# One 2 MB weight load cut into eight spread pieces, and the second group's loads held back behind a transpose

## The chip, the core and the metric

The kernel runs on one core of one Trainium2 chip. The metric is the device time of one execution in microseconds (us), as the median of several executions; for a program on one core that is the time of this core. The engines are TensorE (PE in the profile; PEld is its weight loads), VectorE (DVE), ScalarE (ACT), GpSimd (POOL), and SyncE (SP), whose queue issues nearly all transfers here. Every execution also reports the mean granted TensorE clock, 1.000 being full speed.

## The reference, cut to what matters

Two attention blocks with 2048 tokens, width 1024 and 32 heads, put side by side. Block A is plain softmax attention; block B goes over four segments of 512 tokens with a causal mask, plus a memory that is carried from segment to segment.

```python
qkv = x @ wqkv; p = softmax(q @ k.T * Dh**-0.5); a = (p @ v) @ wo          # A
for s in range(4):                                                          # B
    a_dot = softmax(qs @ ks.T * scale + mask) @ vs
    a_mem = (phi(qs) @ M) / (phi(qs) @ z + 1e-6)
    outs.append(g * a_mem + (1 - g) * a_dot)
    M, z = M + phi(ks).T @ vs, z + phi(ks).sum()
b = concat(outs) @ wo_B
return concat([a, b], axis=-1)
```

## The kernel before

The program does not fix the order of its instructions by hand. Work is described as many small processes; at build, a scheduler plays them against a **model of times** and writes down, for each engine, the order in which the model ran its instructions. That order is then static on the chip. The model has a clock for the transfer queue, too: a transfer of `kb` kilobytes holds it for kb/230 us and is taken to have landed 1.7 us later.

```python
def dispatch(self, eng, t):                  # the scheduler, at build; cut
    ...
    if rq.kb:
        self.dma_free = max(self.dma_free, start + min(cost, 0.6)) + rq.kb / 230
        op.end = max(start + cost, self.dma_free) + 1.7
    ...

def load_WoB(self):                          # B's output weights, before
    yield ("ev", ("pos", self.par["wob"]))   # wob = 60: after 60 steps of the attention
    yield do("SP", lambda e: e.dma_start(self.WoB[:, :, :], self.B_wo.rearrange("(j p) n -> p j n", p=P)),
             w=[("WoB", j) for j in range(NG)], cost=0.6, prio=6, kb=2048)
    self.Q.fire("WoB")
```

The tile WoB serves first as room for early exponentials, so its weights cannot come at the start. `load_WA` and `load_WB` bring 256 KB of projection weights for the next group of heads, `load_xB` 512 rows of B's input through a transposing transfer, and `turn` transposes a V tile (into VA or VB) or the key features of B (into PKt) on the same queue. PKt is read by the matmuls that update the memory (line 942 before, 944 after). The exponentials are line 1112 before, 1114 after; the score matmuls that they wait for are line 1081, then 1083; the matmuls with V are line 1227, then 1229.

## Time and profile before

| what | before |
|---|---|
| median of 3 runs, then of 6 | 1103.65 us, then 1102.97 us |
| all six | 1099.79 to 1105.68 us |
| profiled execution: span, mean clock | 1105.1 us, 0.992 |
| ACT busy, idle | 1078.1 us, 27.0 us |
| WoB load: size, to landing | 2048 KB, 11.7 us |

Idle time of ACT is what there is to win: the span is ACT's busy time plus its idle time.

### The profile page before, as it was taken

The page shows a single profiled execution, that of the slowest core. Times are in us where ns is not written, and L with a number is a line of the kernel's source. Part 1 is how long each engine was busy: PE and PEld are TensorE (multiplying, and loading weights), DVE is VectorE, ACT ScalarE, POOL GpSimd, SP SyncE. Part 2 cuts the span into 40 slices and gives each one's busy share as a digit, 9 for nine tenths or more (in the row PEclk, how much of TensorE's full clock was granted, in tenths as well). Part 3 has the DMA queues.
Part 4 walks back from the last instruction along what each step waited for, and adds up shares of the span by engine and source line. Part 5 has one row for each costly group of instructions (what it writes and reads, how often), then busy time and mean ns, then how long its engine had stood idle before and what let it go on. Part 6 is the DMA issues. An engine that isn't in the chain of part 4 may idle for free.

```text
span 1105.1 us, 54825 instructions
## 1 busy us (share of the span) xinstructions
PE 1045.0 (95%) x25518; PEld 542.3 (49%) x25518; DVE 750.4 (68%) x1573; ACT 1078.1 (98%) x1188; POOL 126.0 (11%) x231
## 2 busy tenths in 40 slices
PE   8899899999999989999999999999999998999998
PEld 4554454544545445454454444445454554554554
DVE  2366547565786978888888798977757768543334
ACT  6999899999999999999999999999999999999997
POOL 2011101101011021110102112211111111100000
PEclk9999899999999999999999999999999999999999
DMA  9722522234302222243212132341142121201011
GB/s 192 98 60 56 126 65 51 53 72 74 74 22 55 61 55 50 46 84 70 60 37 60 36 70 55 65 79 37 46 70 55 37 55 27 84 32 36 32 41 66
DMA packets 213770, 67.53 MB, mean 61 GB/s; under 512 B 202787, under 2 KB 210979, under 8 KB 213539
## 3 DMA queue, kind: packets, MB, share of 16 engines
q1 hardware_dynamic: 212066, 63.07, 27.3%
q8 instruction: 201, 3.29, 1.3%
q10 hardware_dynamic: 1472, 0.92, 0.3%
q14 instruction: 31, 0.25, 0.1%
HBM read 36.70 MB, written 8.39 MB: 41 GB/s over the span
## 4 chain that ended last, share of the span: by engine, by line
ACT 67%; PE 26%; DVE 4%; DMA 1%; issue 1%; ACTq 0%; DVEq 0%
ACT PT L1112 66%; PE ps L726 12%; PE ps L1227 6%; PE ps L1081 5%; PE ps L1322 2%; DMA WA<-in_A_wqkv_dram 1%; DVE OD L1275 1%; ACT OTA L1112 1%; DMA VA<-VT 0%; DVE VT L731 0%; DVE PT L1122 0%; DMA VB<-VT 0%; DVE PH L1150 0%; DVE we L1149 0%; ACT OTB L1112 0%
## 5 line engine op out<-in xcount | busy, mean ns | idle before, releaser
L1112 ACT ACTIVATE PT<-ps 128x1024 bf16<-128x1024 f32 x1164 | 1056.9, 1166 | 10.4 <-PE ps L1081 9.7
L1227 PE MATMUL ps<-PT,ones 128*32 128x256 bf16 (+2 forms) x4784 | 284.1, 269 | 0.0
L1227 PE MATMUL ps<-PT,VA 128*32 128x256 bf16 x4016 | 241.6, 274 | 5.1 <-issue 2.4
L1081 PE MATMUL ps<-QA,KA 32*128 32x256 bf16 x4096 | 211.1, 274 | 30.2 <-ACT PT L1112 25.3
L726 PE MATMUL ps<-xA,WA 128*32 128x512 bf16 (+2 forms) x3424 | 204.9, 359 | 3.9 <-issue 1.3
L726 PE MATMUL ps<-xB,WB 128*32 128x512 bf16 (+1 forms) x3120 | 205.8, 380 | 2.8 <-DVE KA L731 0.8
L1081 PEld LDWEIGHTS ps<-QA,KA 32*128 32x128 bf16 x4096 | 62.9, 92 | 203.6 <-ACT PT L1112 188.1
L1227 PEld LDWEIGHTS ps<-PT,ones 128*32 128x32 bf16 x4784 | 128.4, 97 | 32.0 <-issue 16.4
L1227 PEld LDWEIGHTS ps<-PT,VA 128*32 128x32 bf16 x4016 | 107.4, 96 | 41.2 <-issue 22.8
L726 PEld LDWEIGHTS ps<-xA,WA 128*32 128x32 bf16 x3424 | 77.0, 96 | 78.5 <-issue 28.5
L726 PEld LDWEIGHTS ps<-xB,WB 128*32 128x32 bf16 x3120 | 71.8, 96 | 76.9 <-issue 32.4
L1275 DVE COPY OD<-ps 128x512 f32<-128x512 f32 x127 | 86.7, 683 | 29.5 <-PE ps L1227 28.7
L731 DVE CAST VT<-ps 128x512 bf16<-128x512 f32 x64 | 44.1, 689 | 75.6 <-PE ps L726 68.4
L1327 DVE CAST outsb<-ps 128x512 bf16<-128x512 f32 x56 | 38.7, 690 | 79.1 <-PE ps L1322 76.9
L1124 POOL TENSOR_TENSOR PT<-PT,mask 128x256 bf16<-128x256 bf16 x64 | 46.7, 730 | 352.3 <-ACT PT L1112 351.3
L731 DVE CAST KQB<-ps 128x512 bf16<-128x512 f32 x64 | 44.0, 687 | 44.1 <-PE ps L726 43.8
L1322 PE MATMUL ps<-WoB,OTB 128*32 128x512 bf16 (+1 forms) x1044 | 67.6, 377 | 0.5 <-DVE KQB L731 0.4
L868 POOL COPY VZ<-VB 64x256 bf16<-64x256 bf16 x64 | 29.8, 465 | 318.3 <-DMA VB<-VT 284.2
L1281 DVE STREAM_TRANSPOSE OD<-Rall 128x256 f32<-128x256 f32 x127 | 55.8, 440 | 2.9
L1278 DVE STREAM_TRANSPOSE Dt<-OD 128x256 f32<-128x256 f32 x127 | 55.3, 437 | 2.3
L1322 PE MATMUL ps<-xA,OTA 128*32 128x512 bf16 x836 | 53.3, 379 | 0.0
L1227 PE MATMUL ps<-PT,VB 128*32 128x192 bf16 (+2 forms) x768 | 45.7, 245 | 6.5 <-DVE OD L1275 4.5
(111 smaller groups left out, 888.3 us busy)
## 6 DMA issues: line engine op xcount, KB each, us to landing
WB<-in_B_wk_dram SPq DMA_DIRECT2D x32, 256.0 KB, 3.0
WB<-in_B_wq_dram SPq DMA_DIRECT2D x32, 256.0 KB, 2.9
WB<-in_B_wv_dram SPq DMA_DIRECT2D x32, 256.0 KB, 3.3
out_dram<-outsb SPq DMA_DIRECT2D x63, 128.0 KB, 1.8
WA<-in_A_wqkv_dram SPq DMA_DIRECT2D x23, 256.0 KB, 3.2
WoB<-in_B_wo_dram SPq DMA_DIRECT2D x1, 2048.0 KB, 11.7
xA<-in_A_wo_dram SPq DMA_DIRECT2D x1, 2048.0 KB, 9.5
OTA<-in_A_x_dram SPq DMA_DIRECT2D x2, 256.0 KB, 4.7
```

What stands on the lines that cost most here:

```text
L726: ins = e.matmul(self.ps[32 * c:32 * c + 32, bank, lo:hi], W[:, i, 32 * c:32 * c + 32], x(i)[:, lo:hi], start=st, stop=sp)
L731: return e.tensor_copy(dst, self.ps[:, bank, 0:n])
L868: yield do("POOL", lambda e, j=j: e.tensor_copy(self.VZ[H * j:H * j + H, j:4:2, :], V[0:H, j:4:2, 0:P]), r=[("VB", n % 2)], w=["VZ"], cost ...
L1081: ins = e.matmul(out, l, r, start=a, stop=z)
L1112: yield do("ACT", lambda e: e.activation(to, self.ps[:, pr[0]:pr[1] + 1, 0:n], ACTF.Exp, scale=sc), r=[("ps", bk) for bk in pr], w=keys, c ...
L1124: yield do("POOL", lambda e: e.tensor_tensor(d, d, m, ALU.mult), r=keys + ["mask"], w=keys, cost=0.4 + sz * 0.0014, prio=0)
L1227: ins = e.matmul(out, l, r, start=st, stop=sp)
L1275: yield do("DVE", lambda e: e.tensor_copy(OD[:, :], self.ps[:, OB, :]), r=[("ps", OB)], w=[("OD", x), ("Rb", x)], cost=dve(2 * QU), prio=0 ...
L1278: yield do("DVE", lambda e: e.transpose(Dt[:, :], Rb), r=[("Rb", x)], w=[("Dt", x)], cost=dve(QU), prio=self.par["fp"], hold=0.15)
L1281: yield do("DVE", lambda e: e.transpose(Rb.rearrange("p (a b) -> p a b", b=32), self.spread(Rc)), r=[("Rc", ui % 64)], w=[("Rb", x)], cost ...
L1322: ins = e.matmul(self.ps[32 * c:32 * c + 32, bank, lo:hi], lhs(j)[:, 32 * c:32 * c + 32], W(j)[:, lo:hi], start=st, stop=sp)
L1327: return f(self.outsb[ob][:, :], self.ps[:, bank, :])
```

## The change

Its intent is to keep the transfer queue from filling up: WoB comes in eight pieces of 256 KB, six steps apart, and the loads of the second group, with B's first ones, wait until the last V transpose of the first group has been issued.

```diff
-    par = dict(..., wob=60, mg=0.05, ...)
+    par = dict(..., wob=60, wobs=6, mg=0.05, ...)
-    def load_WA(self, k, g, prio=5, via="SP"):
+    def load_WA(self, k, g, prio=5, via="SP", after=None):
+        if after:
+            yield ("ev", after)
...
-                Q.spawn(self.load_WA(k, g + 1))
+                Q.spawn(self.load_WA(k, g + 1, after=("VA", 0, 3)))
...
     def load_WoB(self):
-        yield ("ev", ("pos", self.par["wob"]))
-        yield do("SP", lambda e: e.dma_start(self.WoB[:, :, :], ...), w=[("WoB", j) for j in range(NG)], cost=0.6, prio=6, kb=2048)
+        src = self.B_wo.rearrange("(j p) n -> p j n", p=P)
+        for j in range(NG):
+            yield ("ev", ("pos", self.par["wob"] + self.par["wobs"] * j))
+            yield do("SP", lambda e, j=j: e.dma_start(self.WoB[:, j, :], src[:, j, :]), w=[("WoB", j)], cost=0.6, prio=6, kb=256)
         self.Q.fire("WoB")
...
         def later():
             yield ("ev", ("pos", self.par["bpos"]))
+            yield ("ev", ("VA", 0, 3))
             for k in range(3):
                 yield from self.load_WB(k, 0)
```

More of the change, by code (lines that the diff above doesn't have):

```diff
@@ L405 @@
 class Kernel:
-    par = dict(b=(16, 12, 9), mem=0, memM=2, span=60, rate=0.6, ahead=28, sl=7, pv=14, ob=4, lead=6, b0=1, bpos=16, wob=60, mg=0.05, off=0, oks=(1, 4, 6), sh=4, pd=6, o0=4, od=0, run=4, po=(1, 1), fp=2, fil=0.65, fs=0.15, ta=2, td=40, pvw=3, pvs=3, slk=0.2, pat=0.0, kh=3, xp=0, wm=1, mk=(0, 1, 1), mp=0, pe=3, tk=(0.5, 1))
+    par = dict(b=(16, 12, 9), mem=0, memM=2, span=60, rate=0.6, ahead=28, sl=7, pv=14, ob=4, lead=6, b0=1, bpos=16, wob=60, wobs=6, mg=0.05, off=0, oks=(1, 4, 6), sh=4, pd=6, o0=4, od=0, run=4, po=(1, 1), fp=2, fil=0.65, fs=0.15, ta=2, td=40, pvw=3, pvs=3, slk=0.2, pat=0.0, kh=3, xp=0, wm=1, mk=(0, 1, 1), mp=0, pe=3, tk=(0.5, 1))
     def __init__(self, nc, A_x, A_wqkv, A_wo, B_x, B_wq, B_wk, B_wv, B_wo, B_beta, out):
@@ L1579, in load_WoB @@
     def load_WoB(self):
-        yield ("ev", ("pos", self.par["wob"]))
-        yield do("SP", lambda e: e.dma_start(self.WoB[:, :, :], self.B_wo.rearrange("(j p) n -> p j n", p=P)),
-                 w=[("WoB", j) for j in range(NG)], cost=0.6, prio=6, kb=2048)
+        src = self.B_wo.rearrange("(j p) n -> p j n", p=P)
+        for j in range(NG):
+            yield ("ev", ("pos", self.par["wob"] + self.par["wobs"] * j))
+            yield do("SP", lambda e, j=j: e.dma_start(self.WoB[:, j, :], src[:, j, :]), w=[("WoB", j)], cost=0.6, prio=6, kb=256)
         self.Q.fire("WoB")
```

## The prediction

The forecast's sum: 5.45 + 0.91 - 0.8 = 5.56 us off 1103.65, which gave 1098.1.

> **What bounds the kernel now.** I read the page first (busy time, chain, costliest groups), then the list of who waited for whom on ScalarE (ACT), then the timeline around each ACT gap, then a table of stretches and the DMA view for the same microseconds.
>
> ```profile
> PE 1045.0 (95%) x25518; PEld 542.3 (49%) x25518; DVE 750.4 (68%) x1573; ACT 1078.1 (98%) x1188; POOL 126.0 (11%) x231
> ...
> ACT 67%; PE 26%; DVE 4%; DMA 1%; issue 1%; ACTq 0%; DVEq 0%
> ...
> L1112 ACT ACTIVATE PT<-ps 128x1024 bf16<-128x1024 f32 x1164 | 1056.9, 1166 | 10.4 <-PE ps L1081 9.7
> ```
>
> ACT is busy 1078.1 of a span of 1105.1 us, nearly all of it in the exponentials of line 1112. The third line says that its own idle time before those 1164 instructions is only 10.4 us, so the most that any change of loads can win is small. The chain names TensorE (PE) for 26%, because PE is 95% busy and the two take turns, but ACT is the one that hardly ever stops. All ACT idle is 1105.1 - 1078.1 = 27.0 us. From the timeline: the start holds 2.51 + 5.53 + 1.90 + 0.35 = 10.3 us (first loads), the end about 6.2 us (last projections and the last store). That leaves about 10.5 us in the middle, and the two places that the change touches hold most of it. First place, the ACT timeline (start, length, last column idle before it):
>
> ```profile
> 123.56 3.08 ACT L1112 ACTIVATE PT<-ps 128x1024 bf16<-128x1024 f32 x3
> 129.80 3.40 ACT L1112 ACTIVATE PT<-ps 128x1024 bf16<-128x1024 f32 x4 [3.15 <-PE ps L1081]
> 133.96 1.94 ACT L1112 ACTIVATE PT<-ps 128x1024 bf16<-128x1024 f32 x2 [0.76 <-PE ps L1081]
> 136.37 3.89 ACT L1112 ACTIVATE PT<-ps 128x1024 bf16<-128x1024 f32 x4 [0.47 <-PE ps L1081]
> 141.34 9.39 ACT L1112 ACTIVATE PT<-ps 128x1024 bf16<-128x1024 f32 x10 [1.07 <-PE ps L1081]
> ```
>
> The exponential before the second line ended at 126.65; ACT then stands 3.15 us, and again 0.76, 0.47 and 1.07 until 141.34: 5.45 us together. All of them wait for score matmuls of line 1081. Why these were late, from the timeline of all engines:
>
> ```profile
> 117.80 0.69 SPq L1581 DMA_DIRECT2D WoB<-in_B_wo_dram  x1
> ...
> 125.06 0.28 PE L1227 MATMUL ps<-PT,VA 128*32 128x256 bf16 x2
> ...
> 127.53 1.85 SPq L737 DMA_TRANSPOSE VA<-VT  x1
> 127.74 0.40 PE L1227 MATMUL ps<-PT,VA 128*32 128x256 bf16 x2 [2.40 <-issue]
> ```
>
> Line 1581 is the one 2 MB load of B's output weights (WoB). Seven and a half microseconds later PE stands 2.40 us inside a group of four matmuls that the program issues with no wait between them, only ahead of the first. So no buffer and no transfer of data is being waited for: the profile calls it "issue", and I read it as PE having no next instruction. The stretches (columns: PE, weight loads, VectorE, ACT, GpSimd busy; granted clock; DMA share; GB/s) show what goes with it:
>
> ```profile
> 118.00:121.00 3.00, 3.00 (x88) 1.78 (x84) 2.93 (x5) 3.00 (x5) 1.30 (x2) 1.00 1.09 226
> 121.00:124.00 3.00, 3.00 (x84) 1.68 (x72) 0.10 (x1) 3.00 (x5) 0.00 (x0) 1.00 0.94 338
> 124.00:127.50 3.50, 1.34 (x34) 0.61 (x31) 0.69 (x1) 2.65 (x3) 1.33 (x2) 0.96 1.18 345
> 127.50:132.00 4.50, 3.29 (x63) 2.27 (x65) 2.45 (x7) 2.20 (x3) 0.28 (x1) 0.50 1.05 59
> 132.00:136.00 4.00, 3.20 (x76) 1.42 (x68) 2.45 (x6) 3.14 (x4) 0.22 (x1) 0.50 0.00 1
> 136.00:142.00 6.00, 6.00 (x116) 2.61 (x112) 3.07 (x9) 4.54 (x5) 0.00 (x0) 0.59 0.01 3
> 142.00:150.00 8.00, 8.00 (x212) 4.61 (x200) 2.78 (x6) 7.98 (x10) 0.00 (x0) 1.00 0.39 86
> ```
>
> DMA is full from 118 to beyond 127.5, up to 345 GB/s. PE does 1.34 us of work in 3.50. Then the granted clock is 0.50 for over 8 us, where the same matmuls take longer (0.61 us for a batch of eight score matmuls against 0.40), and ACT gets 2.20 of 4.50, 3.14 of 4.00, 4.54 of 6.00. From 142 on all is as before. The DMA view of 112 to 140 us:
>
> ```profile
> q8 instruction: 4, 0.07, 1.0%
> ...
> WoB<-in_B_wo_dram SPq DMA_DIRECT2D x1, 2048.0 KB, 11.7
> ...
> WB<-in_B_wk_dram SPq DMA_DIRECT2D x1, 256.0 KB, 11.1
> ```
>
> Another 256 KB load of that window took 11.1 us to land, against a median of 3.0 for its kind on the page. Second place, the first V:
>
> ```profile
> 32.55 0.38 SPq L532 DMA_DIRECT2D WA<-in_A_wqkv_dram  x1
> ...
> 33.28 1.19 SPq L737 DMA_TRANSPOSE VA<-VT  x1
> ...
> 38.26 0.29 PE L1227 MATMUL ps<-PT,VA 128*32 128x256 bf16 x4 [1.13 <-DMA VA<-VT]
> ```
>
> The second group's WA load is put ahead of the last transpose of the first V, more loads follow it, the transpose takes 4.84 us to land (a piece of the chain) instead of the 2.4 of the fastest of its kind, and PE stands 1.13 us for it at 38.26. ACT's next exponential starts 0.91 us late (38.93).
>
> [...]201 packets of 3.29 MB on the instruction queue, 16.4 KB each. [...]the trace shows only that DMA was full when PE stood still. [...](2048 KB in 11.7 us, eight times 256 KB at 3.0 us would be 24), but rate is not what is short here. [...]
>
> **The change part by part.** (1) WoB in eight. Removed: one issue of 0.69 us on the sync queue. Added: eight of about 0.4 to 0.6 us (as the WB loads, 0.37 to 0.58), on a queue that only issues transfers. Bytes are the same. The pieces go at positions 60, 66, ..., 102. A position is two exponentials, bar those of B: 60 positions had passed at 117.8 us, and the whole order has 64 x 8 + 32 x 3 = 608 positions in about 1090 us, 1.79 us each; so one piece each 11 us and the last at 117.8 + 42 x 1.79 = 193 us. WoB is first read at 287.2 us: 90 us to spare. Each piece should land in some 3 us. What it takes off the path: the stop at 125 us (3.15) and the half clock after it (2.30), 5.45 us of ACT. Since every engine's order is fixed at build, what ACT gains at 141 us stays gained unless a later wait takes it. (2) The holding back. The WA load at 32.55 and the WB and xB loads of later wait for the issue of the last V transpose (33.28), so they move by a microsecond or less. The transpose then lands nearer 2.4 to 3.5 us, before 37 us, when PE has finished its earlier work (36.85 + 0.28). Gain 0.91 us of ACT. xB lands about 49 us and its user has no gap near it, so a microsecond there is free. Both parts together: 5.45 + 0.91 = 6.36 us, from 1103.65 to 1097.3. I take back 0.8 us for new small collisions (below): 1098.1.
>
> **Rivals.** (a) The stall stays. At position 60 the first piece still goes out together with three loads of 256 KB and two transposes within 6 us; if these alone starve PE, the time stays near 1102.7 (only part 2 pays). Against it: the load of A's output weights at 950 us is also 2 MB, lands in 9.5 us, and ACT is busy 22.00 of 22.00 us from 948 to 970. So a load of 2 MB alone is survived, and it takes 2 MB plus the bunch; with 256 KB in its stead the bunch is 1 MB. I give this 12%. (b) The pieces hit others. Eight more loads of 3 us among the transposes of V, whose landing PE waits for; each such hit could cost up to the 0.91 seen at 38 us, and two or three of them 2 us: about 1099.5. Some 20%. (c) The order moves. The program places instructions by its own model of engine and DMA times at build; another load plan there changes the order of PE and VectorE work after 117 us. ACT has 2.13 us of gaps at 396 to 401 us behind VectorE, and gaps of such kind may vanish or arise: plus or minus 2 us. (d) PE is the real bound, and the 5.45 us would come back as waits on PE. Against it: from 142 us on ACT stands still for 0.16 us only until 300 us, although PE had fallen behind by the same stop.
>
> **Range and chances.** The floor is busy time plus start and end, 1078.1 + 10.3 + 6.2 = 1094.6 of span, about 1093 for the median, which was 1.5 below the span. The other side is rival (a) with noise: the three runs of before spread from 1099.79 to 1105.68. So 1093.5 to 1102.8 holds it 8 times in 10. Faster by over 2% would need 22 us, more than ACT can give: 1%. Slower by over 2% would need a stall that nothing hints at: 1%.
>
> **What would show it.** Right: no ACT gap over 0.5 us between 100 and 200 us, the granted clock 1.00 there, no PE stop by "issue" inside a group, eight WoB loads with a median landing near 3 us, and no ACT gap at 38 us; ACT busy still about 1078 and its idle time near 20 to 21 us. Wrong: the gap near 125 us with only one piece under way (rival a), fresh gaps behind VA or VB transposes (b), or gaps at other places behind VectorE (c). The prediction is wrong above all if the PE stop has nothing to do with the load.

## The result, and the profile after

The changed kernel took 1101.97 us (median of 6, 1100.72 to 1104.20) against 1102.97 for the kernel before. The ratio is 0.9993, with a 95% interval of 0.9974 to 1.0013. A ratio here is the mean time of one kernel's fast runs over that of the other's in the same rounds, so it is not quite the ratio of the medians. Of the 5.5 us that I forecast not more than about 1 is there.

And yet the profile after looks just as it was predicted to. From the page of the changed kernel (busy times; the chain that ended last; the exponentials with the idle time before them):

```profile
PE 1038.3 (94%) x25434; PEld 539.3 (49%) x25434; DVE 749.2 (68%) x1573; ACT 1078.1 (98%) x1188; POOL 126.1 (11%) x231
...
ACT 62%; PE 27%; DVE 8%; DMA 3%; issue 1%; SPq 0%; DVEq 0%
...
L1114 ACT ACTIVATE PT<-ps 128x1024 bf16<-128x1024 f32 x1164 | 1056.8, 1165 | 4.5 <-PE ps L1083 3.8
```

ACT is busy 1078.1 us as before, and its idle time before exponentials fell from 10.4 to 4.5 us. The span is 1099.0, which is 6.1 less. The stretches around the first WoB piece (columns: stretch, length, busy PE, PEld, DVE, ACT, POOL, granted clock, DMA share, GB/s):

```profile
124.00:127.50 3.50, 3.10 (x88) 1.88 (x84) 2.81 (x7) 3.50 (x6) 1.37 (x3) 1.00 0.20 42
127.50:132.00 4.50, 4.17 (x104) 1.84 (x96) 3.55 (x9) 4.50 (x7) 0.38 (x1) 1.00 0.49 120
132.00:136.00 4.00, 3.79 (x108) 1.95 (x104) 3.37 (x8) 4.00 (x5) 0.00 (x0) 1.00 0.46 101
```

PE works 3.10 of 3.50 us where it had worked 1.34, ACT all of them, the clock stays at 1.00 and DMA is at a half or less. Comparing these two profiles would have told the predicted story to the end: 6.1 us gained. The timed runs of the same two kernels say otherwise. So the question for the experiments is which of the two profiles is not typical, and what else differs.

### The profile page after: what moved, and what is told of

The parts are those of the page before. It is cut to its first block, busy times and chain, and to the rows that moved or that the text cites. A ratio compares the mean times of both kernels' runs of the same rounds, so it can differ in the third digit from the quotient of the medians.

```text
span 1099.0 us, 54671 instructions
## 1 busy us (share of the span) xinstructions
PE 1038.3 (94%) x25434; PEld 539.3 (49%) x25434; DVE 749.2 (68%) x1573; ACT 1078.1 (98%) x1188; POOL 126.1 (11%) x231
## 4 chain that ended last, share of the span: by engine, by line
ACT 62%; PE 27%; DVE 8%; DMA 3%; issue 1%; SPq 0%; DVEq 0%
ACT PT L1114 61%; PE ps L728 11%; PE ps L1229 6%; PE ps L1083 5%; PE ps L1324 3%; DMA xB<-in_B_x_dram 1%; DMA VA<-VT 1%; DMA PKt<-PH 1%; DVE VT L733 1%; DVE PH L1152 1%; DVE we L1151 1%; DVE PH L899 1%; DVE OD L1277 1%; DVE we L1150 1%; ACT OTA L1114 1%
## 5 line engine op out<-in xcount | busy, mean ns | idle before, releaser
L728 PE MATMUL ps<-xB,WB 128*32 128x512 bf16 x3096 | 203.6, 379 | 3.6 <-DMA xB<-in_B_x_dram 1.1
```

Source lines behind the costliest of these rows:

```text
L728: ins = e.matmul(self.ps[32 * c:32 * c + 32, bank, lo:hi], W[:, i, 32 * c:32 * c + 32], x(i)[:, lo:hi], start=st, stop=sp)
```

## The experiments

Twelve runs were made on the chip, all beside runs of the kernel before. **Theory 1** is the prediction's: the stop of PE near 125 us belongs to the 2 MB load and comes in every execution. **Theory 2**: its length is a matter of chance, and the profile that I read had caught a long one. A third possibility, the prediction's rival (c), is that the changed load plan makes the build write a different order, and that this order costs something elsewhere (theory A below).

### Is the stop always there? The kernel before once more, and each half alone

b_again is the kernel before, a_again the changed one. split_only leaves out the two lines of holding back; hold_only keeps them and puts the one 2 MB load back. The orders were compared instruction by instruction: hold_only has exactly the order of the kernel before on PE, ACT, DVE and POOL, split_only exactly that of the changed kernel. Only the transfers differ within each pair.

```diff
# split_only, against the changed kernel
-                Q.spawn(self.load_WA(k, g + 1, after=("VA", 0, 3)))
+                Q.spawn(self.load_WA(k, g + 1))
-            yield ("ev", ("VA", 0, 3))
# hold_only, against the changed kernel: load_WoB as before (one load, kb=2048)
```

> The kernel before once more, to see whether the 2.40 us stop of PE near 125 us and the half clock after it are there in every execution. Theory 1 (the stop belongs to the load and comes every time): every run shows a mean granted clock near 0.992, the profile shows ACT gaps of about 5.4 us between 126 and 142 us, ratio 1.000. Theory 2 (the stop is a matter of chance and comes in some executions): clocks of the runs differ, from 0.992 to 0.998, the time falls as the clock rises, and the profile may lack the gap.

> The changed kernel once more. Theory 1: clock 0.997 to 0.998 in all runs, no ACT gap over 1 us after 25 us, ratio to before 0.994 to 0.995. Theory 2 (chance stops in both): the mean ratio stays near 0.999, with runs of 1099 to 1100 at clock 0.998 and runs of 1102 to 1104 at 0.995, which means that other stops than the one of the load come in this kernel too.

> The eight spread pieces alone, without the holding back. The order of PE, ACT and DVE is the same as in the changed kernel, only the sync queue differs. Both theories: the ACT gap of about 0.9 us at 38 us is back and adds 0.9 us to the changed kernel. Theory 1: ratio to before 0.995. Theory 2: ratio 1.000 within 0.002.

> The holding back alone, with the one load of 2 MB. Both theories: no ACT gap at 38 us, 0.9 us less than before, ratio 0.999. Theory 1: the stop near 125 us is there in the profile and the clock is 0.992 in every run. Theory 2: the clocks of the runs differ as with the kernel before.

| run | median, range (us) | ratio to before, 95% | clocks of its runs |
|---|---|---|---|
| b_again | 1101.00, 1099.51 to 1105.21 | 1.0002, 0.9975 to 1.0030 | 0.994 to 1.000 |
| a_again | 1101.43, 1100.28 to 1102.44 | 0.9997, 0.9972 to 1.0022 | 0.997 to 0.998 |
| split_only | 1101.88, 1099.78 to 1103.58 | 1.0003, 0.9977 to 1.0029 | 0.995 to 0.998 |
| hold_only | 1098.94, 1097.34 to 1103.05 | 0.9974, 0.9948 to 1.0000 | 0.995 to 1.000 |

Theory 1 falls. The kernel before has runs of 1099.5 us at clock 1.000 and runs of 1105.2 at 0.994, and in these rounds one of 1108.28 at 0.992. The clocks can be read as a count: in the profiles the clock records show 0.50 for 3.41 us (once in the changed kernel's), or for two or four times that in one piece (6.8 us in hold_only, 13.65 in the first profile), and one such stretch lowers a mean over 1100 us by 0.0016. By an estimate from these numbers 0.998 means one stretch, 0.997 two, 0.995 three, 0.994 four and 0.992 five. Of the 39 runs of the kernel before in this set of rounds and the two below, the five with none took 1099.75 us in the mean, the six with four 1104.97. The profile that I had read has five, four of them in one piece from 127.25 us, at the stop.

Two expectations missed as well. The gap at 38 us was to come back in split_only with 0.9 us and to be absent in hold_only; from 35 to 41 us ACT lacked 0.31 us in the one and 0.62 in the other. And hold_only's 0.26% is three times the 0.9 us expected, at the edge of noise; it was not followed up.

The second profile of the kernel before has a span of 1097.8, less than the changed kernel's. Here is the place of the stop in that second profile (start, length, instruction, idle before it):

```profile
126.23 0.29 PE L1227 MATMUL ps<-PT,VA 128*32 128x256 bf16 x2 [0.32 <-issue]
...
127.44 1.02 ACT L1112 ACTIVATE PT<-ps 128x1024 bf16<-128x1024 f32 x1 [0.22 <-PE ps L1081]
```

PE stands again, inside the same group of four matmuls, but for 0.32 us instead of 2.40; ACT loses 0.22 us instead of 5.45, and the clock does not drop. hold_only, with the same order and the same load, stood 1.7 us there. The reading as a missing next instruction can be checked in the traces' own records. Counted in order of start, PE stops after its instruction 5825 in each of these three. An instruction block of 16 KB as the instruction queue moves it (201 packets, 3.29 MB) was close to 256 instructions (51262 PE instructions in 201 blocks), and 5825 is 22 x 256 + 193. Short stops at 11 and 16 us (0.72 and 0.58 us in the first profile) come after instructions 449 = 256 + 193 and 705 = 2 x 256 + 193. So these stops of PE are where, by this count, one block ends and the next begins. When was the missing block moved? From the DMA view of the kernel before, in the first profile, 121 to 125 us (the whole count of packets, then the queue of ordinary transfers; the instruction queue, q8, has no line at all):

```profile
DMA packets 693, 1.42 MB, mean 355 GB/s; under 512 B 0, under 2 KB 0, under 8 KB 693
...
q1 hardware_dynamic: 693, 1.42, 97.2%
```

And the next 1.5 us:

```profile
q1 hardware_dynamic: 629, 0.52, 104.2%
q8 instruction: 1, 0.02, 4.4%
```

While 1.42 MB went by, no instruction packet did; one is recorded at 125.17 us, when PE had already started its last instruction before the stop (125.06). When it was asked for the trace does not show. Over all profiles the picture is the same. The previous block was used up (instruction 5569) near 120 us; from there to the start of the fetch it took 5.12, 3.27 and 3.27 us in three profiles of the kernel before (the third is the single look below) and 4.59 in hold_only, against 0.66 to 1.23 us in the eight profiles of kernels with the spread load (over all 200 block ends of the first profile the median is 0.56 us). This block lasted PE 5.0 us in the first profile. After the delays of 0.66 to 1.23 us no stop is seen at its end, after those of 3.3 to 5.1 us stops of 0.6 to 2.7 us between two instructions' starts. What decides between 3.3 and 5.1 was not found. A last profile of the kernel before, alone, was taken to see one more stop:

> One more profile of the kernel before, for the length of the PE stop after its instruction 5825 (so far 2.67, 0.59 and, with the holding back, 1.98 us from one start to the next). If its length is a matter of chance between executions[...], it will again be another: somewhere from 0 to 3 us, with a fetch of the next block that starts 2 to 5.5 us after the block before was used up, against 0.7 to 1.2 us in all kernels with the spread load.

It took 1100.09 us and stopped 0.61 us at that place. So in three profiles of the kernel before, the loss of ACT between 100 and 160 us was 5.49, 0.22 and 0.24 us, and 2.77 in hold_only: 2.2 us in the mean of four, not 5.45.

Theory 2 explains the first profile. It does not explain why the changed kernel, which has that stop in no profile, isn't at 1099. hold_only, which may have it, is even the faster. The order is left.

### Order and load taken apart

The order was frozen: the scheduler still sees one transfer of 2048 KB and so writes the order of the kernel before, and only afterwards the load is cut, with pieces 1 to 7 put 12 exponentials apart. That is split_old_order, and hold_split_old_order with the holding back. one_new_order does the reverse: the changed kernel's order, but the first piece brings all 2 MB at once (the later ones are cut to 16 KB each; the result is right). load_more puts 1.5 MB of useless loads ahead of the 2 MB one. All four were checked to have exactly the order of PE, ACT, DVE and POOL that they claim.

```diff
# split_old_order, against the kernel before (deps and semaphores of the new pieces cut)
+        self.wob_op = yield do("SP", lambda e: e.dma_start(self.WoB[:, 0, :], src[:, 0, :]), w=[...], cost=0.6, prio=6, kb=2048)
+    def spread_WoB(self):                    # called when the order is complete
+        acts = [o for o in R.all[i0:] if o.ex == "ACT"]
+        for j in range(1, NG):
+            o = Op(f"D{23 + j}", 0, lambda e, j=j: e.dma_start(self.WoB[:, j, :], src[:, j, :]))
+            R.all.insert(R.all.index(acts[12 * j - 1]) + 1, o)
# one_new_order, against split_only
-  e.dma_start(self.WoB[:, j, :], src[:, j, :])
+  e.dma_start(self.WoB[:, :, :], src) if j == 0 else e.dma_start(self.WoB[:, j, 0:64], src[:, j, 0:64])
# load_more, against the kernel before: ten loads of 128 or 256 KB into amem, tB, outsb ahead of WoB, cost 0 in the model
```

> The eight spread pieces, but in the exact order of PE, ACT and VectorE of the kernel before: the order is made with the one load, and only then the load is cut. Theory A (what the change gains by the spread load it loses by the new order): no PE stop near 125 us, clock 0.998 to 1.000 in nearly all runs, time near 1100.0, ratio to before 0.998 to 0.999 and about 1 us under the changed order with the same load. Rival B (the spread load itself brings fresh collisions): time as split_only, 1101 to 1102, ratio 1.000.

> Both parts of the change in the order of the kernel before. Theory A: the 0.5 to 0.9 us of the holding back on top, time 1097.3 to 1098.5, ratio 0.996 to 0.997: the best of all. Rival B: 1100 to 1101.

> The one 2 MB load in the changed order (the seven later pieces are cut to 16 KB each, so that the order stays; result unchanged). Theory A: PE stops again after its instruction 5825 near 124 us, where its next block of instructions starts, for 0.3 to 2.5 us, runs spread as before's do, and the mean is 1 to 2 us over split_only, ratio 1.001 to 1.002. Rival C (the stop has nothing to do with the load): no difference to split_only in time or spread.

> The kernel before with 1.5 MB of useless loads put ahead of the 2 MB one, into tiles not used before 200 us; order of PE, ACT and VectorE as before. Theory A (a full queue delays the block of instructions): the stop after PE instruction 5825 is there in every run and longer, 2.5 to 6 us, clock 0.990 to 0.994, time 1104 to 1110, ratio 1.003 to 1.008. Rival C: as before, ratio 1.000.

| run | median, range (us) | ratio to before, 95% | clocks |
|---|---|---|---|
| split_old_order | 1099.89, 1098.70 to 1102.62 | 0.9980, 0.9959 to 1.0002 | 0.997 to 1.000 |
| hold_split_old_order | 1098.98, 1097.46 to 1099.67 | 0.9968, 0.9949 to 0.9988 | 0.998 to 1.000 |
| one_new_order | 1108.69, 1107.53 to 1109.72 | 1.0061, 1.0041 to 1.0081 | 0.992 to 0.995 |
| load_more | 1104.55, 1102.15 to 1105.40 | 1.0016, 0.9989 to 1.0043 | 0.997 to 0.998 |

In the old order the same two parts of the change take 0.32% off, clear of noise in these rounds; in the new order they take off nothing that can be seen. So the new order costs about what the change gains. Where, is told by ACT's busy time (the fourth of the busy times) in two stretches. The changed kernel, then the frozen order with both parts:

```profile
100.00:160.00 60.00, 58.44 (x1404) 30.22 (x1402) 35.65 (x73) 59.93 (x68) 5.55 (x10) 1.00 0.38 82
200.00:520.00 320.00, 297.19 (x7384) 154.42 (x7380) 239.96 (x505) 316.96 (x351) 40.53 (x71) 0.99 0.30 59
```

```profile
100.00:160.00 60.00, 57.14 (x1412) 30.12 (x1408) 33.08 (x67) 60.00 (x68) 4.46 (x8) 1.00 0.35 79
200.00:520.00 320.00, 300.65 (x7524) 156.67 (x7520) 244.28 (x512) 319.02 (x353) 40.01 (x71) 1.00 0.29 60
```

From 100 to 160 us both are as good as full, as any kernel with the spread load was (missing 0.00 to 0.25 us in seven profiles). From 200 to 520 us the changed kernel lacks 3.04 of 320 us, the frozen one 0.98. Over all profiles ACT got 316.08 to 317.19 us there in the changed order (five profiles, mean 316.59) and 317.31 to 319.02 in the old (eight, mean 318.39): 1.8 us. And what PE waits for in the changed order, from its list of waits (us in total, times, longest):

```profile
PE ps L944 <- DMA PKt<-PH: 2.5, 4, 1.3
...
PE ps L728 <- DMA xB<-in_B_x_dram: 1.1, 1, 1.1
```

The same list for the frozen order (the line is 946 there) has this and no wait for xB:

```profile
PE ps L946 <- DMA PKt<-PH: 0.5, 1, 0.5
```

In four profiles with the changed order and the spread load PE waits 2.5 to 3.9 us in all for the landing of PKt, and in three of them 0.5 to 1.2 us for xB; in seven profiles with the old order and no added loads it is 0.0 to 0.6 us for PKt and none for xB is listed. One such wait in the changed kernel, with the exponential that it delays:

```profile
213.75 0.41 PE L944 MATMUL ps<-VB,PKt 128*32 128x129 bf16 x16 [1.29 <-DMA PKt<-PH]
...
214.83 1.94 ACT L1114 ACTIVATE PT<-ps 128x1024 bf16<-128x1024 f32 x2 [0.37 <-PE ps L1083]
```

The reason fits the code: the model takes a transfer to land 1.7 us after its queue is free. With 2048 KB on that queue the model pushes everything behind it back by 8.9 us, with 256 KB only by 1.1, and the order it writes afterwards is another; the first difference on PE is that a memory-update matmul that reads PKt stands earlier. On the chip PKt then took 4.0 us to land (the transfer for the wait just shown). What these waits cost is told by ACT's own gaps between 200 and 520 us. The changed kernel after the gap just shown, then the frozen order:

```profile
250.20 16.34 ACT L1114 ACTIVATE PT<-ps 128x1024 bf16<-128x1024 f32 x18 [0.74 <-PE ps L1083]
...
390.75 100.02 ACT L1114 ACTIVATE PT<-ps 128x1024 bf16<-128x1024 f32 x110 [0.57 <-PE ps L1083]
491.63 29.01 ACT L1114 ACTIVATE PT<-ps 128x1024 bf16<-128x1024 f32 x32 [0.86 <-PE ps L1083]
```

```profile
390.31 116.06 ACT L1116 ACTIVATE PT<-ps 128x1024 bf16<-128x1024 f32 x128 [0.60 <-PE ps L1085]
506.57 13.86 ACT L1116 ACTIVATE PT<-ps 128x1024 bf16<-128x1024 f32 x15 [0.20 <-PE ps L1085]
```

The 0.37 us at 214.83 follow the PKt wait, the 0.86 at 491.63 the wait for xB (1.08 us of PE at 489.56). The 0.57 at 390.75 stand behind VectorE, and the frozen order has them too. The 0.74 at 250.20 follow no transfer: PE had only short waits, for ACT, and then one stretch at half clock in which it got less done than ACT needed.

```profile
244.13:247.55 3.42, 1.98 (x56) 1.17 (x56) 2.16 (x6) 3.42 (x5) 1.34 (x2) 1.00 0.55 117
247.55:250.96 3.41, 3.41 (x61) 1.31 (x60) 1.18 (x4) 2.67 (x4) 0.51 (x1) 0.50 0.02 5
```

In the four profiles of the changed order with the spread load, ACT's gaps after the PKt wait at 214 us are 0.23 to 0.64 us (mean 0.40), at the xB wait 0 to 1.01 (mean 0.54), in or just after stretches at half clock 0.74 to 2.30 (mean about 1.5; of a_again's 1.75 us at 391.31 the 0.58 that others lose there is not counted). So half clock is the largest part, and PKt the smallest. The timed runs point the same way: all 24 runs of the changed order with the spread load (after, a_again, a_third, split_only) have a clock of 0.998 or less, thus at least one stretch, 1.75 in the mean; of the 18 runs with the spread load in the frozen order six have none, and the mean is 0.78. Why the changed order has more of them was not tested.

**one_new_order** came out in the direction expected, yet more than three times the size that I had put, and the block stop is only 0.3 us of it. The largest part is this wait, and the half clock that comes with it (three to five stretches in its six runs):

```profile
129.91 0.63 PE L944 MATMUL ps<-VB,PKt 128*32 128x129 bf16 x16 [3.70 <-DMA PKt<-PH]
...
132.38 1.51 ACT L1114 ACTIVATE PT<-ps 128x512 bf16<-128x512 f32 x2 [4.19 <-PE ps L1083]
```

The order made for a free queue has the PKt matmul early; with the 2 MB load in fact on the queue, PKt takes 9.3 us to land, PE waits 3.70 us, and ACT 4.19. So in the changed order the spread load is worth 6.7 us (mean 1108.65 against 1101.94 of split_only, in other rounds, where the kernel before had nearly the same mean), in the old order 2.0 (mean of before 1102.01 against 1100.04, same rounds). What the transfer's shape is worth depended here on the order it met.

**load_more** missed. The time is not told from that of the kernel before (1.0016, within noise), and the stop after instruction 5825 was gone: the fetch started only 1.89 us after the block before it was used up. That was at 121.70 us, before the 2 MB load was issued (123.7), so the 2 MB load cannot have held it up. But the next two blocks, used up at 124.8 and 131.0 us with the 2 MB on the queue, were fetched after 1.6 and 2.7 us, also sooner than the 3.3 to 5.1 above. What PE waited for instead was PKt again:

```profile
136.62 0.63 PE L942 MATMUL ps<-VB,PKt 128*32 128x129 bf16 x16 [5.04 <-DMA PKt<-PH]
...
137.85 1.94 ACT L1112 ACTIVATE PT<-ps 128x1024 bf16<-128x1024 f32 x2 [4.53 <-PE ps L1081]
```

So in these runs the delay of a fetch does not simply grow with the bytes on the queue. What it depends on stays open.

### The same chip, and a try to mend the model

Since the comparison of orders lay in two sets of rounds, both kernels were run together. after_pk tells the model that PKt lands 1.5 us later, so that its matmuls are placed later.

```diff
-            op.end = max(start + cost, self.dma_free) + 1.7
+            op.end = max(start + cost, self.dma_free) + (3.2 if rq.tail == 2.5 else 1.7)
-            yield self.turn(self.PKt[:, :, :], PH[:, 0, :], [("PH", b)], ["PKt"])
+            pk = self.turn(self.PKt[:, :, :], PH[:, 0, :], [("PH", b)], ["PKt"])
+            pk[1].tail = 2.5
+            yield pk
```

> The changed kernel on the same chip as the next two. Theory A (its gain is given back by waits of PE that its new order brings): time near 1101.3 to 1102.2, 3 to 4 waits of PE for the landing of PKt, 2.5 us in total, one for xB.

> Both parts in the order of the kernel before, again. Theory A: 1098.5 to 1099.5, 2 to 3 us under the changed kernel on the same chip, PE waits for PKt under 0.7 us in total. If it were chance (rival D) the two would lie within 1 us.

> The changed kernel, whose model of times at build is told that the PKt transposes land 1.5 us later, so that it places the matmuls that read PKt later. Theory A: waits of PE for PKt fall from 2.5 to under 1 us, time 1099.5 to 1100.5, ratio to before 0.998. Rival D (the waits are not what costs): 1101.3 to 1102.2 still. A new order may bring waits of its own at other places, which the profile will show.

| run | median, range (us) | ratio to before, 95% |
|---|---|---|
| a_third (the changed kernel) | 1101.79, 1100.46 to 1107.43 | 1.0015, 0.9991 to 1.0039 |
| hold_split_third (frozen order) | 1099.92, 1098.65 to 1101.10 | 0.9993, 0.9976 to 1.0010 |
| after_pk | 1112.89, 1111.73 to 1115.65 | 1.0114, 1.0094 to 1.0133 |

The frozen order is 1.9 us under the changed kernel by the medians, a little short of the 2 to 3 expected; of its six runs only two are slower than the changed kernel's fastest. So the order's cost stands on one chip. Against the kernel before the frozen order is less clear this time, 0.9993. Its mean ratio over both sets of rounds is 0.998, no better than hold_only (0.9974) or split_old_order (0.9980) in one set each; whether it beats the kernel before at all is not settled, since the second interval includes 1. after_pk failed as a remedy and is instructive as a failure. Its waits for PKt are gone from the list, just as meant; yet the new order has a hole elsewhere, in one place nearly four times as long as all that it was to save:

```profile
827.46 1.94 ACT L1116 ACTIVATE PT<-ps 128x1024 bf16<-128x1024 f32 x2 [6.98 <-PE ps L1085]
```

ACT stands 6.98 us there, since the masked copy of B's keys (KZ), which the score matmuls need, comes only at 824 us, after a late projection of the keys. Every change to the model draws a new order, and orders differ by more than the waits that one aims at.

## Why the prediction was right or wrong

- **What bounds the kernel: right.** ACT stays at 1078.1 us busy in both profiles (1077.0 to 1078.8 in all fourteen, whose spans go from 1096.9 to 1111.2), so nearly every change of time is a change of its idle time.
- **The mechanism of the stop: right in the main.** As I read the traces, PE lacked its next block of instructions: it stops where a block ends, the fetch is seen 3.3 to 5.1 us after the block before was used up, against 0.7 to 1.2 with the spread load, and in the same order of instructions it stops there in all four profiles with the one load and in none of three with the spread pieces (in none of eight over all orders). That a full queue is enough to delay a fetch is not shown: load_more had more on it and no stop. Rival (a), that the stall stays, did not happen, nor did rival (b), that the pieces cost more than they gain: in the old order they gain 2.0 us by the means (0.9980, at the edge of noise). But the changed kernel is not free of slow executions: one of its timed runs took 1107.43 us with five stretches at half clock, and no profile shows where.
- **The size of part 1: wrong, and this is the first failed step.** "What it takes off the path: the stop at 125 us (3.15) and the half clock after it (2.30), 5.45 us of ACT." That was the length in one execution, slower than the six timed beside it, and the sum took it off the median of three others. Taken off its own 1106.82 us, the 6.36 us of both parts give 1100.5, and the changed kernel's profiled execution took 1100.72. In the four profiles with the one load in the old order ACT lost 5.49, 0.22, 0.24 and 2.77 us from 100 to 160 us, and with the spread load 0.09 in the mean of seven. The term is 2.2 - 0.1 = 2.1 us, as far as four profiles tell.
- **The gain stays gained: wrong, and this is the second.** "Since every engine's order is fixed at build, what ACT gains at 141 us stays gained unless a later wait takes it" holds for one order. But the change makes the build write another one, and that loses 1.8 us between 200 and 520 us, as time at half clock and as waits for xB and PKt. The prediction named this as rival (c) with plus or minus 2 us, and then left it out of the sum.
- **Part 2: right in kind, too large.** Predicted were a landing in 2.4 to 3.5 us and 0.91 us of ACT. The transpose took 4.0 us in the changed kernel's profile: the held WA load goes out at 34.32 us, right behind its issue (33.08) and before its landing (37.07), so I take the two to have shared the queue. From 35 to 41 us ACT lacked 0.58 us in the mean of seven profiles without the holding back and 0.24 in six with it (after_pk, of a third order, left out), so the term is 0.3 us.
- **The range.** The floor of 1093 rests on the median being "1.5 below the span", which compares the span of one execution with the times of others. In every profile the time is 1.7 to 1.8 us above its own span, so the floor would be 1096.3. The measured 1101.97 is inside the range, but at the end drawn for rival (a), which did not happen: that is luck.
- **The sum.** 2.1 + 0.3 - 1.8 = 0.6 us by these terms, where 5.5 was predicted. The three sets of rounds say 0.9993, 0.9997 and 1.0015, each within about 0.2%: no gain that can be told from none.

## What to carry to other kernels

A stop in one profile is one draw: before a wait is priced, look at the spread of the timed runs and their clocks, and at a second profile, above all if the profiled run is among the slow ones. And take a loss off the time of the execution in which it was read. Where the order of instructions comes from a model that is fed with transfer sizes, every change of a load is also a change of order; freeze the order and change only the load before you credit or blame the load. And look at what lands behind a long transfer: with the 2 MB load on the queue PKt took 9.3 to 11.8 us (one_new_order, the kernel before, load_more) where its median in the kernel before is 2.9, and a block of instructions was fetched up to 5.1 us after the one before it was used up.

## What the traces show of fetches, the clock and small transfers

- Instruction fetch. With the one 2 MB load in the order of the kernel before, the fetch started 3.3 to 5.1 us after the block before was used up, instead of 0.7 to 1.2, and PE, which used up that block in 5.0 us in the first profile, stopped for 0.6 to 2.7 us. A late fetch is seen without that load, too: in the first profile, while a transposing load of xB (issued at 247.87 us, landed 9.0 us later) was on the queue, the next fetch came 4.72 us after instruction 11457 (249.87 us), and PE's stop at the following block end, from one start to the next, was 0.48 us.
- Clock. In the first profile 13.65 us at 0.50 began at 127.25 us, within the stop of 2.40 us (125.34 to 127.74); in b_again a stop of 0.32 us at the same place came with none; in the changed kernel 3.41 us at 0.50 came from 247.55 us, after short waits. I cut the profiles of the kernel before and of the changed kernel into windows of 3.41 us in step with their clock records. Their three stretches at half clock come after windows in which PE was busy for 1.50, 1.20 (before, from 123.84 and 393.49 us) and 1.98 us (changed, from 244.14). After the one other window with less than 2 us of work (1.86, before, from 11.20) the clock stayed at 1.00. What decides was not shown.
- Small transposing transfers. PKt landed in 11.1 us behind the 2 MB load, against a median of 2.9 us in the same kernel.
